# A top-2 router behind linear attention: expert work regrouped from blocks of 128 slots to pairs of 256, with a seven-product second layer

## The chip, the cores and the metric

The kernel runs on one core of one Trainium2 chip. The metric is the device time of one execution in microseconds. The time before is 727.77 us, the median of three runs (725.59 to 728.99). The profile is of one more execution and spans 730.0 us from its first to its last instruction. TensorE does matrix products (the profile splits it into PE, the matmuls, and PEld, the loads of the stationary operand), VectorE (DVE) and ScalarE (ACT) do elementwise work, GpSimd (POOL) here mostly issues indirect transfers, and SyncE (SP) issues the other transfers.

## The reference

Attention with a decaying state comes first, then a layer of eight experts in which each token goes to two. All data are float32.

```python
batch, n_heads, seq, head_dim = (4, 8, 768, 48)
N, D, E, F = (3072, 384, 8, 1024)
# attention
f = 1.0 / (1.0 + np.exp(-f_logit))
for t in range(S):
    state = f[:, :, t, :, None] * state + np.einsum('bhd,bhe->bhde', k[:, :, t], v[:, :, t])
    y[:, :, t] = np.einsum('bhd,bhde->bhe', q[:, :, t], state)
# x: (batch * seq, heads * head_dim)
noisy_logits = x @ w_gate + np.log1p(np.exp(x @ w_noise)) * noise
top2 = np.argpartition(-noisy_logits, 2, axis=1)[:, :2]
# top2_w: softmax over the two
for e in range(E):
    for k in range(2):
        mask = top2[:, k] == e
        h = np.maximum(x[mask] @ w1[e], 0.0)
        out[mask] += top2_w[mask, k, None] * (h @ w2[e])
```

3072 tokens with two experts each make 6144 slots. Each slot needs a first layer of 384 x 1024 and a second of 1024 x 384.

## The kernel before

Attention works on 24 samples (six chunks of 128 positions times four batches), and each sample passes through seven stages in a pipeline. The features `x` of each sample are written to `x_rows` in DRAM. After every four samples the router finds the two experts of each token and writes an entry (token, weight) into the list of each expert, also in DRAM. When half of the tokens are routed, `plan("a", ...)` lays out the first 17 blocks of 128 slots (`NA`) by full lists, so that expert work can start before the rest is routed; `plan("b", ...)` lays out the rest. A remainder of at most 64 slots becomes a half block. The program holds a fixed number of blocks and four half blocks (`NH`), and a conditional part at the end for what does not fit into them.

The loads of `f`, `q`, `k` and `v` go into rings of buffers that are given back when attention is over:

```python
RING = {"f": 5, "q": 4, "k": 4, "v": 6}
pads = {n: [ld.tile([C, H, DP], F32, tag=f"{n}{i}", name=f"{n}{i}") for i in range(RING[n])] for n in "fqkv"}
```

One block of 128 slots; `KO` is 3, `FO` is 8 and `NR` is 2 (two buffers for the weights of each layer, loaded only where the expert changes, `cond=new`):

```python
def turned(t):
    xp = one_bank(f"xgp{t}")
    for i in range(KO):
        nc.tensor.transpose(xp[:, i * 128:(i + 1) * 128], xg[t][:, i * 128:(i + 1) * 128], ident)
    xt[t] = ffn.tile([128, KO, 128], F32, tag="xt", name=f"xt{t}")
    nc.vector.tensor_copy(xt[t], xp[:, 0:DM].rearrange("d (k t) -> d k t", k=KO))

def block_of(t, end=NB - NT):
    ahead("fetch", min(t + 5, end))        # the list entries of the block
    ahead("gather", min(t + 4, end))       # the rows of x they name
    hs = ffn.tile([128, FO, 128], F32, tag="hs", name=f"hs{t}")
    for half in range(2):
        hp = one_bank(f"hp{t}_{half}").rearrange("f (o t) -> f o t", t=128)
        for o in range(FO // 2):
            fo = half * (FO // 2) + o
            for i in range(KO):
                nc.tensor.matmul(hp[:, o, :], lhsT=w1[t % NR][:, i, fo * 128:(fo + 1) * 128],
                                 rhs=xt[t][:, i, :], start=(i == 0), stop=(i == KO - 1))       # L838
        nc.scalar.activation(hs[:, half * (FO // 2):(half + 1) * (FO // 2), :], hp, AF.Relu)   # L840
        if half == 0:
            yield
    ahead(1, min(t + NR + 1, end))         # w1 of a later block
    if t + 1 < end:
        turned(t + 1)
    yield
    yp = one_bank(f"yp{t}")
    for fo in range(FO):
        nc.tensor.matmul(yp[:, 0:DM], lhsT=hs[:, fo, :], rhs=w2[t % NR][:, fo, :],
                         start=(fo == 0), stop=(fo == FO - 1))                                 # L849
        # ... one yield in the middle
    ahead(2, min(t + NR + 1, end))         # w2 of a later block
    ys = ffn.tile([128, DM], F32, tag="ys", name=f"ys{t}")
    nc.vector.tensor_scalar(ys, yp[:, 0:DM], slots[t][:, 1:2].bitcast(F32), None, ALU.mult)    # L855
    nc.gpsimd.indirect_dma_start(out=out, ..., in_=ys, ..., compute_op=ALU.add)                # L856
```

The last line adds the block's rows to `out`, so `out` has to be zeroed first. That is done during attention, one or two row groups per sample:

```python
elif stage is output:
    for m in (n - 2,) if 2 <= n < 18 else (2 * n - 20, 2 * n - 19) if 18 <= n < 22 else ():
        nc.sync.dma_start(out=out[m * 128:(m + 1) * 128, :], in_=zero)
```

The first loads for the experts are spread over turns of the driving loop by a generator, once the first half's entries are written:

```python
for what, until in (("", 6), ("fetch", 2), ("fetch", 4), (1, 1), ("fetch", 5), (2, 1), ("", 4), ("gather", 1),
                    ("gather", 2), (1, 2), ("gather", 3), ("", 3), ("turned", 0), (2, 2), ("gather", 4)):
```

Of the kernel before, what the change touches and what calls it, by code (L numbers as in the profile page):

```python
# [10 lines left out]
F32 = mybir.dt.float32  # L11
# [320 lines left out]
def kernel(  # L332
# [48 lines left out]
    NB = max((2 * N - 65 * n) // 128 + n for n in range(E + 1))  # L381
    NH = 4
    HALF = NCH // 2
    NT = 3
    NA = -(-(2 * HALF * B * C - E * 127) // 128)
# [7 lines left out]
    rest = top.tile([1, 1], I32, tag="rest", name="rest")  # L393
    ctx = whole.enter_context(ExitStack())

    const = ctx.enter_context(tc.tile_pool(name="const", bufs=1))
    rt = ctx.enter_context(tc.tile_pool(name="rt", bufs=2))
    ps2 = ctx.enter_context(tc.tile_pool(name="ps2", bufs=1, space=PSUM))
    ps1 = ctx.enter_context(tc.tile_pool(name="ps1", bufs=6, space=PSUM))
    wk = ctx.enter_context(tc.tile_pool(name="wk", bufs=2))  # L400
    ffn = ctx.enter_context(tc.tile_pool(name="ffn", bufs=3))
    loads = ExitStack()
    ld = loads.enter_context(tc.tile_pool(name="ld", bufs=1))

    def one_bank(name):
        return ps1.tile([128, 512], F32, tag="one", name=name)
# [10 lines left out]
    pads = {n: [ld.tile([C, H, DP], F32, tag=f"{n}{i}", name=f"{n}{i}") for i in range(RING[n])] for n in "fqkv"}  # L417
# [16 lines left out]
    end_of = counting("end_of", [[128, N // 128]], base=128)  # L434
    block = counting("block", [[1, NB]])

# [10 lines left out]
    LR = E * N + 128  # L447
# [42 lines left out]
    xw, puts = [], []  # L490
# [123 lines left out]
    def route(c):  # L614
# [3 lines left out]
        def pause():  # L618
            for _ in range(2 if c < HALF else 1):
                yield  # L620
# [43 lines left out]
        for _ in range(2 if c < HALF else 6):  # L664
            yield from pause()
# [12 lines left out]
        def put(b, r):  # L678
            into = nc.gpsimd.indirect_dma_start(  # L679
# [15 lines left out]
    steer, steer_h = {}, {}  # L695

    def plan(name, n, groups, count):


        def t(shape, tag, dtype=F32):  # L700
            return rt.tile([128] + shape, dtype, tag=tag, name=f"{tag}_{name}", bufs=1)

        total = one_bank(f"total_{name}")[:, 0:E]
        nc.tensor.matmul(total, lhsT=ones, rhs=upto[groups - 1][:, :, B], start=True, stop=True)
        full = t([E, N // 128], "full")
        nc.vector.tensor_tensor(full, total.unsqueeze(2).broadcast_to((128, E, N // 128)),
                                (end_of if count == ALU.is_ge else over_of).unsqueeze(1).broadcast_to((128, E, N // 128)), count)
        yield
        nblk, ends, step = t([E], "nblk"), t([E], "ends"), t([E], "step")
        nc.vector.tensor_reduce(nblk, full, axis=AX.X, op=ALU.add)  # L710
        if count == ALU.is_gt:
            half, first, ends_h = t([E], "half"), t([E], "first"), t([E], "ends_h")
            nc.vector.scalar_tensor_tensor(half, in0=nblk, scalar=128.0, in1=total, op0=ALU.mult, op1=ALU.is_lt)
            nc.vector.scalar_tensor_tensor(first, in0=iota, scalar=float(N // 128), in1=nblk, op0=ALU.mult, op1=ALU.add)
            nc.vector.tensor_tensor_scan(ends_h, data0=ones[:, 0:E], data1=half, initial=0.0, op0=ALU.mult, op1=ALU.add)
        nc.vector.tensor_tensor(nblk, nblk, used[:, 0:E], ALU.subtract)
        nc.vector.tensor_tensor_scan(ends, data0=ones[:, 0:E], data1=nblk, initial=0.0, op0=ALU.mult, op1=ALU.add)
        yield
        if count == ALU.is_gt:
            over = t([1], "over")  # L720
            nc.vector.tensor_scalar(over, ends_h[:, E - 1:E], NH + 0.5, None, ALU.is_gt)
            nc.vector.scalar_tensor_tensor(more, in0=ends[0:1, E - 1:E], scalar=n - NT + 0.5, in1=over[0:1], op0=ALU.is_gt, op1=ALU.max)

        nc.vector.tensor_tensor(step, used[:, 1:E + 1], used[:, 0:E], ALU.subtract)
        nc.vector.tensor_tensor(step, step, nblk, ALU.subtract)
        nc.vector.tensor_scalar(step, step, float(N // 128), None, ALU.add)
        yield
        past = t([NB, E], "past")[:, 0:n, :]
        nc.vector.tensor_tensor(past, block[:, 0:n].unsqueeze(2).broadcast_to((128, n, E)),
                                ends.unsqueeze(1).broadcast_to((128, n, E)), ALU.is_ge)  # L730
        yield
        ex, row, new = t([n], f"ex{n}"), t([n], f"row{n}"), t([n], f"new{n}")
        nc.vector.tensor_reduce(ex, past, axis=AX.X, op=ALU.add)
        nc.vector.tensor_tensor(past, past, step.unsqueeze(1).broadcast_to((128, n, E)), ALU.mult)
        nc.vector.tensor_reduce(row, past, axis=AX.X, op=ALU.add)
        yield
        nc.vector.scalar_tensor_tensor(row, in0=row, scalar=used[:, 0:1], in1=block[:, 0:n], op0=ALU.add, op1=ALU.add)
        nc.vector.tensor_scalar(row, row, float(E * N // 128), 128.0, ALU.min, ALU.mult)
        to = top.tile([128, n, 3], I32, tag=f"steer_{name}", name=f"steer_{name}")
        nc.vector.tensor_copy(to[:, :, 1], row)  # L740
        nc.vector.tensor_scalar(ex, ex, float(E - 1), None, ALU.min)
        nc.vector.tensor_copy(to[:, :, 0], ex)
# [12 lines left out]
        for i in range(n):  # L755
            steer[base + i] = to[0:1, i, :]
# [368 lines left out]
```

## Time and profile before

The table has the groups that the change touches, from the profile of the kernel before. "Mean" is the mean length of one instruction; matmuls overlap their neighbours, so a mean is longer than the distance from one to the next.

| line | engine | what | count | busy us | mean ns |
|---|---|---|---|---|---|
| L838 | PE | first layer, 128 columns | 2304 | 267.7 | 276 |
| L849 | PE | second layer, 384 columns | 768 | 257.3 | 487 |
| L816 | PE | transposes of gathered rows | 144 | 24.0 | 276 |
| L840 | ACT | relu, 128 x 512 | 96 | 57.3 | 597 |
| L818 | DVE | copy of the transposes | 48 | 26.8 | 558 |
| L855 | DVE | scaling by the gate | 48 | 29.6 | 617 |
| L856 | POOL | scatter into `out`, issue | 48 | 76.0 | 1583 |
| L799 | POOL | gather of rows, issue | 48 | 47.9 | 999 |

The weights are 96 conditional loads of 1536 KB each. The zeros are 24 writes of 192 KB. The groups L838 and L849 have 3072 of the 5354 matmul records; an f32 matmul leaves two records. Read the table together with the stretches of the span: the busy shares are means over attention, which ends near 184 us, and over the expert blocks, which begin near 160 us and run to 717 us.

### The profile page before, as it was taken

What the parts mean: (1) busy time and instruction counts of PE and PEld (TensorE: products, weight loads), DVE (VectorE), ACT (ScalarE), POOL (GpSimd) and SP (SyncE); (2) the same over time, 40 slices, a digit from 0 to 9 for tenths busy, and PEclk for the clock granted to TensorE, in tenths of its full rate; (3) what the DMA queues carried; (4) which work ended last, traced back from release to release, by engine and by line L of the source; (5) the groups of instructions that cost most, each with busy time, mean ns of one, the idle gap of its engine ahead of it and who ended that gap; (6) DMA issues with size and microseconds to landing.
All of it is one profiled execution on the core that took longest, in us unless ns stands there. A gap on an engine that the chain in (4) does not pass through costs nothing.

```text
span 730.0 us, 13666 instructions
## 1 busy us (share of the span) xinstructions
PE 699.4 (96%) x5354; PEld 563.0 (77%) x5354; DVE 200.2 (27%) x503; ACT 163.7 (22%) x365; POOL 232.8 (32%) x267
## 2 busy tenths in 40 slices
PE   6999989969999999999999999999999999999992
PEld 5889978858788787787788768876787678767881
DVE  7878887822232250010110110010011001101000
ACT  5766655621111010110010011001110101010100
POOL 5223674421174562122132123312322232312210
PEclk9999999989999999999999999999999999999997
DMA  8889888889997988899839649974997189563211
GB/s 173 151 199 216 166 164 182 165 279 368 373 260 194 251 189 264 282 301 331 276 57 381 195 113 292 351 250 118 302 348 233 26 267 333 161 210 74 34 23 15
DMA packets 179866, 156.41 MB, mean 214 GB/s; under 512 B 116978, under 2 KB 164240, under 8 KB 179792
## 3 DMA queue, kind: packets, MB, share of 16 engines
q1 hardware_dynamic: 167440, 135.91, 62.7%
q0 software_dynamic: 12352, 19.52, 13.2%
q8 instruction: 45, 0.74, 0.4%
q14 instruction: 29, 0.24, 0.1%
HBM read 192.51 MB, written 20.15 MB: 291 GB/s over the span
## 4 chain that ended last, share of the span: by engine, by line
PE 87%; DMA 5%; DVE 3%; ACT 1%; SPq 1%; issue 1%; POOL 0%; POOLq 0%; DVEq 0%; ACTq 0%
PE hp L838 36%; PE yp L849 34%; PE sc L554 3%; PE xgp L816 2%; PE xp L605 2%; PE y L572 2%; PE yp_h L910 1%; PE hp_h L896 1%; DMA k<-in_k_dram 1%; DMA w<-in_moe_w_dram 1%; DMA x_rows<-xs 1%; PE y L583 1%; DVE L L528 1%; PE kp L514 1%; PE kp L548 1%
## 5 line engine op out<-in xcount | busy, mean ns | idle before, releaser
L838 PEld LDWEIGHTS hp<-xt,w 128*128 128x128 f32 x2304 | 264.9, 192 | 15.3 <-issue 3.4
L838 PE MATMUL hp<-xt,w 128*128 128x128 f32 x2304 | 267.7, 276 | 0.4 <-DMA w<-in_moe_w_dram 0.4
L849 PE MATMUL yp<-w,hs 128*128 128x384 f32 x768 | 257.3, 487 | 0.0
L849 PEld LDWEIGHTS yp<-w,hs 128*128 128x128 f32 x768 | 141.7, 190 | 90.0 <-issue 2.6
L856 POOL DMA_INDIRECT out_dram<-ys,slots x48 | 76.0, 1583 | 308.8 <-DVE ys L855 171.4
L840 ACT ACTIVATE hs<-hp 128x512 f32<-128x512 f32 x96 | 57.3, 597 | 455.1 <-PE hp L838 455.1
L818 DVE COPY xt<-xgp 128x384 f32<-128x384 f32 x48 | 26.8, 558 | 236.8 <-PE xgp L816 236.8
L855 DVE TENSOR_SCALAR ys<-yp,slots 128x384 f32<-128x384 f32 x48 | 29.6, 617 | 204.0 <-PE yp L849 199.4
L799 POOL DMA_INDIRECT xg<-x_rows,slots x48 | 47.9, 999 | 35.4 <-DMA slots<-lists 19.1
L679 POOL DMA_INDIRECT lists<-entry,sloti x48 | 47.6, 992 | 12.9 <-issue 9.1
L508 POOL TENSOR_SCALAR f<-f 128x384 f32<-128x384 f32 x22 | 28.0, 1272 | 30.8 <-DMA f<-in_f_logit_dram 17.4
L557 DVE TENSOR_TENSOR A<-sc,causal 128x1024 f32<-128x1024 f32 x24 | 29.3, 1222 | 16.1 <-PE sc L554 15.9
L554 PE MATMUL sc<-qP,kQ 64*128 64x128 f32 x384 | 30.6, 304 | 0.0
L528 DVE TENSOR_TENSOR_SCAN L<-f,cap 128x512 f32<-128x512 f32 x24 | 29.8, 1243 | 2.2 <-ACT cap L523 2.2
L572 PE MATMUL y<-A,v 128*64 128x128 f32 x384 | 28.1, 290 | 1.7 <-DMA v<-in_v_dram 1.4
L816 PE MATMUL xgp<-ident,xg 128*128 128x128 f32 x144 | 24.0, 276 | 5.5 <-DMA xg<-x_rows,slots 5.5
L915 POOL DMA_INDIRECT out_dram<-ys_h,slots_h x8 | 11.4, 1431 | 55.6 <-DVE ys_h L913 48.0
L554 PEld LDWEIGHTS sc<-qP,kQ 64*128 64x128 f32 x384 | 25.7, 204 | 4.3 <-issue 3.8
L605 PE MATMUL xp<-w_rt,yT 128*128 128x112 f32 x192 | 27.2, 284 | 0.0
L572 PEld LDWEIGHTS y<-A,v 128*64 128x64 f32 x384 | 21.9, 143 | 5.6 <-DVE A L557 1.6
L605 PEld LDWEIGHTS xp<-w_rt,yT 128*128 128x128 f32 x192 | 23.3, 191 | 3.6 <-issue 2.2
L587 ACT COPY yT<-y 128x256 f32<-128x256 f32 x48 | 15.5, 376 | 41.7 <-PE y L583 40.3
(169 smaller groups left out, 439.3 us busy)
## 6 DMA issues: line engine op xcount, KB each, us to landing
w<-in_moe_w_dram SPq DMA_DIRECT2D x96, 1536.0 KB
w_h<-in_moe_w_dram SPq DMA_DIRECT2D x8, 1536.0 KB
f<-in_f_logit_dram SPq DMA_DIRECT2D x24, 192.0 KB
q<-in_q_dram SPq DMA_DIRECT2D x24, 192.0 KB
k<-in_k_dram SPq DMA_DIRECT2D x24, 192.0 KB
v<-in_v_dram SPq DMA_DIRECT2D x24, 192.0 KB
x_rows<-xs SPq DMA_DIRECT2D x24, 192.0 KB
out_dram<-zero SPq DMA_DIRECT2D x24, 192.0 KB
```

What stands on the lines that cost most here:

```text
L528: nc.vector.tensor_tensor_scan(L[n], data0=logf[n], data1=cap[n % 2].rearrange("d a t -> d (a t)"), initial=0.0, op0=ALU.add, op1=ALU.min)
L554: nc.tensor.matmul(sc[:, par, cols(hp)], lhsT=kQ[n][rows(par), cols(hp)], rhs=qP[n][rows(par), cols(hp)], start=True, stop=True)
L572: nc.tensor.matmul(at(hp, par), lhsT=vt[:, 2 * hp + par, :], rhs=A[n][:, par, cols(hp)], start=(hp < 2), stop=(c == 0 and hp >= HP - 2))
L605: nc.tensor.matmul(xp[:, hp, :], lhsT=yT[n][:, hp % 2, cols(hp // 2)], rhs=w_rt[:, hp, :], start=True, stop=True)
L679: into = nc.gpsimd.indirect_dma_start(out=lists, out_offset=bass.IndirectOffsetOnAxis(ap=sloti[:, r, b:b + 1], axis=0), in_=entry[:, c, b, ...
L799: nc.gpsimd.indirect_dma_start(out=xg[t], out_offset=None, in_=x_rows[0:HALF * B * C] if t < NA else x_rows, in_offset=bass.IndirectOffset ...
L816: nc.tensor.transpose(xp[:, i * 128:(i + 1) * 128], xg[t][:, i * 128:(i + 1) * 128], ident)
L838: nc.tensor.matmul(hp[:, o, :], lhsT=w1[t % NR][:, i, fo * 128:(fo + 1) * 128], rhs=xt[t][:, i, :], start=(i == 0), stop=(i == KO - 1))
L840: nc.scalar.activation(hs[:, half * (FO // 2):(half + 1) * (FO // 2), :], hp, AF.Relu)
L849: nc.tensor.matmul(yp[:, 0:DM], lhsT=hs[:, fo, :], rhs=w2[t % NR][:, fo, :], start=(fo == 0), stop=(fo == FO - 1))
L855: nc.vector.tensor_scalar(ys, yp[:, 0:DM], slots[t][:, 1:2].bitcast(F32), None, ALU.mult)
L856: nc.gpsimd.indirect_dma_start(out=out, out_offset=bass.IndirectOffsetOnAxis(ap=slots[t][:, 2:3], axis=0), in_=ys, in_offset=None, bounds_ ...
```

## The change

Blocks become pairs of 256 slots. There are 24 of them (`NP`), of which the first five (`NA`) are laid out when half of the tokens are routed. The four half blocks of 64 remain. A remainder of 65 to 192 slots would become a single block of 128 in the conditional part at the end.

The first layer has 256 columns for each matmul. The second layer of a pair is a product of two matrices, each cut into 2 x 2: the activations by halves of the hidden dimension (`f`) and by the two sets of 128 slots (`s`), the weights by halves of the hidden dimension and of the 384 output columns (192 each). Winograd's form of Strassen's method makes it from seven products of the parts instead of eight. It needs four sums of the weights (`u1` to `u4`) and four of the activations (`s1` to `s4`) ahead of the products, and more additions after them. The sums are made on VectorE. The activation sums lie where attention's `f` ring was, the weight sums where the `q` and `k` rings were. The first pair runs while `q` and `k` are still in use, so its weight sums lie in the second buffer of `w1`. The rings become single tiles with a lifetime of the whole program for this.

```diff
+    f_all = ring.tile([C, RING["f"], H, DP], F32, tag="f_all", name="f_all")
+    qk_all = ring.tile([C, RING["q"] + RING["k"], H, DP], F32, tag="qk_all", name="qk_all")
...
+    sm = {i + 1: f_all[:, i].rearrange(...) for i in range(4)}
+    sums_of = [sums(w1[1].rearrange("p k f -> p (k f)")), sums(qk_all.rearrange("p a h d -> p (a h d)"))]
...
-    def block_of(t, end=NB - NT):
+    def pair_of(t):
+        def a(f, s):
+            return hs[:, f * FH:(f + 1) * FH, s * 128:(s + 1) * 128]
+        def b(f, c):
+            return w2[t % NR][:, f * FH:(f + 1) * FH, c * HC:(c + 1) * HC]
+        def mix(*which):
+            for m in which:
+                x, y, op = {"u1": (b(0, 1), b(0, 0), ALU.subtract), "u2": (b(1, 1), u[1], ALU.subtract),
+                            "u3": (b(1, 1), b(0, 1), ALU.subtract), "u4": (b(1, 0), u[2], ALU.subtract),
+                            "s1": (a(0, 1), a(1, 1), ALU.add), "s2": (sm[1], a(0, 0), ALU.subtract),
+                            "s3": (a(0, 0), a(0, 1), ALU.subtract), "s4": (a(1, 0), sm[2], ALU.subtract)}[m]
+                nc.vector.tensor_tensor((u if m[0] == "u" else sm)[int(m[1])], x, y, op)
+        u = sums_of[t > 0]
+        when = [["u3"], ["u1"], ["u2", "s3"] if t else ["u2"], ["u4"]]
+        when += [["s1"], ["s2"], ["s4"]] if t else [["s3", "s1"], ["s2"], ["s4"]]
+        ahead("fetch", t + 5)
+        ahead("gather", t + 3)
+        hs = ffn.tile([128, FO, 256], F32, tag="hs", name=f"hs{t}", bufs=1)
+        for fo in range(0, FO, 2):
+            hp = one_bank(f"hp{t}_{fo}").rearrange("f (o t) -> f o t", o=2)
+            for o in range(2):
+                for i in range(KO):
+                    nc.tensor.matmul(hp[:, o, :], lhsT=w1[t % NR][:, i, ...], rhs=xt[t][:, i, :], ...)
+            nc.scalar.activation(hs[:, fo:fo + 2, :], hp, AF.Relu)
+            mix(*when[fo // 2])
+            if fo == FO - 2 and t:
+                ahead(1, t + NR + 1)
+            yield
+        def product(name, x, y):
+            ...
+            for o in range(FH):
+                nc.tensor.matmul(P[name], lhsT=x[:, o, :], rhs=y[:, o, :], start=(o == 0), stop=(o == FH - 1))
+        product(1, a(0, 0), b(0, 0))
+        ...                                        # mix(*when[4])
+        product(7, sm[3], u[3])
+        nc.scalar.copy(P17.rearrange("t a w -> t (a w)"), bank[0][:, 0:DM])
+        nc.scalar.mul(left[0], P17[:, 0], gate[0])
+        if t + 1 < NP:
+            turned(t + 1, 0)
+        mix(*when[5])
+        yield
+        product(4, a(1, 1), u[4])
+        mix(*when[6])
+        yield
+        product(5, sm[1], u[1])
+        nc.vector.tensor_tensor(left[1], P17[:, 1], P[4], ALU.add)
+        nc.vector.tensor_tensor(right[1], P17[:, 1], P[5], ALU.add)
+        if t + 1 < NP:
+            turned(t + 1, 1)
+        yield
+        product(6, sm[2], u[2])
+        nc.vector.tensor_tensor(mid, P17[:, 0], P[6], ALU.add)
+        for to in (left[1], right[1]):
+            nc.vector.tensor_tensor(to, to, mid, ALU.add)
+        nc.scalar.mul(ys[1], ys[1], gate[1])
+        scatter(1)
+        nc.vector.tensor_tensor(mid, mid, P[5], ALU.add)
+        nc.scalar.mul(right[0], mid, gate[0])
+        yield
+        product(2, a(1, 0), b(1, 0))
+        nc.vector.scalar_tensor_tensor(left[0], in0=P[2], scalar=gate[0], in1=left[0], ...)
+        yield
+        product(3, sm[4], b(1, 1))
+        if not t:
+            ahead(1, NR + 1)
+        ahead(2, t + NR + 1)                       # never ahead of the loads of w1
+        nc.vector.scalar_tensor_tensor(right[0], in0=P[3], scalar=gate[0], in1=right[0], ...)
+        scatter(0)
```

The zeros of the first half's rows are written during attention from sample 8 on, one row group per sample, and those of the second half beside the pairs from pair 1 on, one per piece of a pair. Routing is spread over fewer turns from the second chunk on, and the first loads start from a list of their own:

```diff
-                for m in (n - 2,) if 2 <= n < 18 else (2 * n - 20, 2 * n - 19) if 18 <= n < 22 else ():
-                    nc.sync.dma_start(out=out[m * 128:(m + 1) * 128, :], in_=zero)
+                if 8 <= n < 8 + NS // 2:
+                    zeros(1)
...
-            for _ in range(2 if c < HALF else 1):
+            for _ in range(2 if c == 0 else 1):
...
+        for what, until in (("", 13), ("fetch", 1), (1, 1), ("fetch", 2), ("fetch", 3), (2, 1), ("gather", 1), ("gather", 2),
+                            ("fetch", 4), ("gather", 3), ("fetch", 5), ("turned", 0)):
...
+            for _ in range(2 if i >= NS - 1 else 1):
+                if done["turned"] and (n_first < 5 or i >= NS - 3 and stage is not forget) and (n_first < 11 or i >= NS - 1):
+                    next(pairs)
+                    n_first += 1
```

A pair has eleven pieces (one per `yield`). With the last condition up to two pairs are begun while the last samples of attention still run. After attention its buffers in PSUM are given back[...].

## The prediction

> **What bounds the kernel now.** I read the busy line, the row of 40 slices and the chain of work that ended last first, because together they say whether one engine sets the time.
>
> ```profile
> PE 699.4 (96%) x5354; PEld 563.0 (77%) x5354; DVE 200.2 (27%) x503; ACT 163.7 (22%) x365; POOL 232.8 (32%) x267
> ...
> PE   6999989969999999999999999999999999999992
> ...
> PE 87%; DMA 5%; DVE 3%; ACT 1%; SPq 1%; issue 1%; POOL 0%; POOLq 0%; DVEq 0%; ACTq 0%
> ```
>
> TensorE is busy for 96% of the span and is 87% of the chain. "Busy" is an average, so next I cut the span into stages (columns after the stretch: its length, then PE, PEld, DVE, ACT and POOL busy us, granted clock, DMA share, GB/s):
>
> ```profile
> 20.00:100.00 80.00, 77.67 (x1105) 70.49 (x1104) 64.60 (x140) 55.48 (x145) 33.38 (x43) 1.00 0.88 188
> 100.00:150.00 50.00, 44.69 (x604) 39.25 (x602) 38.05 (x91) 29.29 (x73) 25.43 (x41) 0.97 0.83 164
> 150.00:160.00 10.00, 6.62 (x60) 5.45 (x61) 2.01 (x3) 0.65 (x2) 3.57 (x4) 0.66 0.89 286
> 160.00:340.00 180.00, 180.00 (x1183) 145.84 (x1184) 39.25 (x158) 24.49 (x52) 64.07 (x78) 1.00 0.94 282
> 340.00:717.00 377.00, 377.00 (x2291) 290.23 (x2289) 40.59 (x71) 42.96 (x72) 94.79 (x73) 1.00 0.66 202
> 717.00:730.00 13.00, 0.19 (x1) 0.00 (x0) 0.62 (x1) 0.00 (x0) 1.56 (x1) 0.65 0.15 19
> ```
>
> From 160 to 717 us, 557 us, TensorE has no gap: the expert blocks are bound by it, and only fewer or shorter matmuls shorten them. Before 160 us attention runs, with VectorE (64.60 of 80) and DMA (share 0.88) close behind; here there are gaps. The last 13 us are the last block's scatter and the end of the program.
>
> TensorE's own timeline in the bound stretch (start, length, line, count) gives the price of a block:
>
> ```profile
> 342.99 5.52 PE L838 MATMUL hp<-xt,w 128*128 128x128 f32 x48
> 348.35 0.49 PE L816 MATMUL xgp<-ident,xg 128*128 128x128 f32 x3
> 348.67 5.33 PE L849 MATMUL yp<-w,hs 128*128 128x384 f32 x16
> 353.84 5.52 PE L838 MATMUL hp<-xt,w 128*128 128x128 f32 x48
> ```
>
> Differences of starts: first layer 348.35-342.99 = 5.36 us, transposes 0.32, second layer 5.17, one block 10.85. One f32 matmul is two records (24 matmuls, 48 records), so a record of 128 columns takes 5.36/48 = 111.7 ns and one of 384 columns 5.17/16 = 323 ns. Those two are the ruler for everything below.
>
> Last, the end of attention, where the gaps are:
>
> ```profile
> 146.87 0.60 PE L514 MATMUL kp<-ident,k 128*128 128x128 f32 x4
> 152.94 0.87 PE L816 MATMUL xgp<-ident,xg 128*128 128x128 f32 x3 [5.47 <-DMA xg<-x_rows,slots]
> 153.74 2.08 PE L554 MATMUL sc<-qP,kQ 64*128 64x128 f32 x16
> ...
> 159.87 2.92 PE L838 MATMUL hp<-xt,w 128*128 128x128 f32 x24 [0.44 <-DMA w<-in_moe_w_dram]
> 162.72 1.16 PE L554 MATMUL sc<-qP,kQ 64*128 64x128 f32 x16
> ```
>
> The first block's gather arrives 5.47 us late, and afterwards the same 16 score records take 2.08 us instead of 1.16.
>
> [...] The 2.08 against 1.16 us and the clock of 0.66 agree: a gap costs more than itself. [...] The trace has 689 ns for the 512 elements of qP[...] and 1222 for the 1024 of the masked scores[...]. [...]
>
> **The change part by part.** The work fits: from the reference's inputs the eight experts get 766, 738, 811, 777, 800, 755, 719 and 778 slots, which by the new rule are 3 pairs each and 4 half blocks, exactly 24 pairs and 4 halves. The 48 blocks and 4 halves of the trace become the same slots, and the fallback stays unused.
>
> *First layer.* 24 matmuls of 256 columns in place of 48 of 128. Between my two points a column costs (323-111.7)/256 = 0.825 ns, so a record of 256 takes 217 ns, and a pair 48 x 217 = 10.4 us against 2 x 5.36 = 10.7. Saves 0.3.
>
> *Second layer.* Eight products of four 192-column matmuls per pair (that is what 16 matmuls of 384 columns are) become seven: 28 matmuls, 56 records of 111.7 + 64 x 0.825 = 164.5 ns, 9.2 us against 10.34. Saves 1.1. Columns alone would save 1/8, 1.28; twice as many records give 0.15 back.
>
> *Transposes* stay, 0.65 per pair. A pair: 10.4 + 9.2 + 0.65 = 20.3 us against 21.7. **24 x 1.4 = 34 us saved**, all of it in the gapless stretch or taking its place.
>
> *Sums around the products.* VectorE per pair: four weight sums of 768 elements, [...]3.8; four activation sums of 512, 0.69 each, 2.8; two copies of 0.56, 1.1; eight operations on 192 columns at about 0.35 (the trace's 192-element copy takes 0.345), 2.8. Together 10.5 us in 20.3. ScalarE: four activations of 0.6 plus copies, about 4. Both lie beside TensorE. Latency also fits: weight sums need only w2 and run during the first layer; the s1 sum is ready about 1.7 us after the last first-layer matmul (copy-out 0.6, sum 0.7, waits), while its product starts after three others, 3.9 us later. Price on the path: 0 to 0.2 us per pair.
>
> *Zeros and the start of the experts.* Twelve of the 24 zero writes leave attention. Routing of the first half also takes fewer turns; counting turns of the driving loop, the fetch of the first list moves from near sample 21 to sample 19 and the first transposes come 12 turns (about 1.6 samples, 9.5 us) after it. Before, the first fetch is issued at 147.11 us, next to the 146.87 us end above, so the data could not be there. I expect the gap of 5.5 us and its slow clock (0.9 for the scores, 0.9 for the outputs that follow) mostly to go, and perhaps part of a 2.0 us wait for k at 109 us. **About 7 of 11 us saved.**
>
> *First pair's sums in w1[1].* So pair 1's w1 can be loaded only after the first pair's sixth product. In program order about 7 us of TensorE work lies between that and pair 1. A 1.5 MB weight load takes 4.2 us at the 368 to 373 GB/s that the two best early slices show, and took 8.77 us when it was contended at 151 us. **I charge 3 us** here, with the slower restart.
>
> *End.* Before: VectorE scaling 0.62, scatter issue 1.56, landing. After: a VectorE operation on 192 columns, then the same scatter; the other half's scatter was issued a product earlier. 0.
>
> Sum: 727.8 - 34 - 7 + 3 = 690; with the small terms rounded, **689 us**.
>
> **Rivals.** *A: the sums hold up the products.* If a sum came late in each pair, by 1 to 1.5 us, the 34 us would shrink to nothing: 715 to 720. For it: VectorE goes from a tenth of the late stretch (40.59 of 377) to half,[...] and its queue mixes copies that wait for TensorE with sums that TensorE needs. Against: two to three microseconds of margin in the order above. *B: the weights become the wait.* w1[1] is held by sums, loads of w2 are held back behind those of w1, and four loads come together after pair 0. For it: 8.77 us in the chain for one load before. If the four loads run at a contended pace, TensorE idles 10 to 15 us around pair 1: 700. Later it is unlikely: fewer loads than before (21 expert changes by my count against about 30) and 20 us per pair to land them. *C: attention gains nothing from fewer zeros*, because its other traffic is as heavy: 696. *D: the layers gain as reckoned, and all stalls of the start go*: 680.
>
> **Range and chances.** The 34 us rest on measured record times and a full TensorE; interpolation is good to 2 ns on 2496 records, 5 us. The start may be off by 8. That gives 677 to 705. Faster by over 2% means below 713.2: only A does otherwise. Faster 0.94, within 2% 0.05, slower 0.01.
>
> **What would show it.** Right: second-layer records near 164 ns, 56 to a pair, pair period 20.2 to 20.5 us between first-layer starts, TensorE without gaps after attention, VectorE near 50% in the pairs, no wait above 1 us for xg at the first pair. Wrong: TensorE waiting on VectorE sums in every pair (A), a wait on w of several us at pair 1 (B), or records of 192 columns well above 165 ns. A repeated wait of over 1.4 us per pair would refute the prediction.

## The result and the profile after

The changed kernel takes **706.14 us** (median, 704.01 to 706.79) against 728.38 us (725.59 to 729.51) of the kernel before in the same measurement: a ratio of **0.9695, interval 0.9659 to 0.9731**. It is faster, by 22.2 us. The prediction said 689.

First the busy line, the row of 40 slices and the chain that ended last, from the page of the changed kernel:

```profile
PE 667.0 (95%) x4778; PEld 598.9 (85%) x4778; DVE 383.3 (55%) x860; ACT 208.7 (30%) x461; POOL 239.4 (34%) x267
...
PE   6999989979999989999999999999999999999992
...
issue 12%; DMA 4%; POOL 2%; POOLq 0%
```

TensorE is as full as before, and VectorE has gone from 27% to 55%. The chain breaks off after 18% of the span here, so it says nothing of the rest, and the readings below rest on stretches and timelines.

The stretches of the changed kernel (length, then PE, PEld, DVE, ACT and POOL busy us, granted clock, DMA share, GB/s):

```profile
20.00:100.00 80.00, 77.72 (x1100) 70.19 (x1100) 62.23 (x136) 53.91 (x140) 34.18 (x47) 1.00 0.94 200
100.00:140.00 40.00, 35.76 (x451) 31.92 (x451) 32.90 (x108) 22.18 (x58) 21.83 (x34) 0.91 0.72 144
140.00:150.00 10.00, 6.16 (x82) 5.62 (x83) 5.45 (x12) 4.73 (x12) 5.67 (x8) 0.93 1.02 377
...
160.00:260.00 100.00, 95.96 (x656) 87.19 (x654) 59.39 (x187) 23.62 (x55) 35.90 (x49) 0.98 0.60 182
260.00:400.00 140.00, 140.00 (x759) 126.35 (x758) 67.79 (x127) 29.16 (x54) 45.04 (x34) 1.00 0.77 242
400.00:689.00 289.00, 289.00 (x1579) 258.90 (x1578) 136.46 (x249) 60.78 (x114) 75.30 (x57) 1.00 0.54 157
```

From 260 us on TensorE has no gap. But the stretch of 160 to 260 us, which was full before, has lost 4 us to gaps. Gaps and a lowered granted clock are there from 100 to 160 us as they were before (0.91 from 100 to 140 us and 0.83 from 140 to 160; before, 0.97 from 100 to 150 and 0.66 from 150 to 160). Attention now ends near 211 us, where it ended near 184. TensorE's timeline gives a pair, where it is gapless:

```profile
300.23 10.52 PE L880 MATMUL hp<-xt,w 128*128 128x256 f32 x48
310.59 1.46 PE L894 MATMUL y<-w,hs 128*128 128x192 f32 x8
311.89 1.46 PE L894 MATMUL y<-qk_all,f_all 128*128 128x192 f32 x8
313.19 0.49 PE L839 MATMUL xgp<-ident,xg 128*128 128x128 f32 x3
...
320.35 10.52 PE L880 MATMUL hp<-xt,w 128*128 128x256 f32 x48
```

First layer 310.59 - 300.23 = 10.36 us, one product 1.30, transposes 0.33 twice, **one pair 20.12 us**, against two blocks of 10.85, 21.70, before. A record of 256 columns thus takes 10.36/48 = 215.8 ns and one of 192 columns 1.30/8 = 162.5. The line through these two, 53.3 ns for 64 columns, gives 322.4 ns at 384 columns and 109.2 at 128, where the kernel before took 323 and 111.7.

The sums' groups on the page (count, then busy us, mean ns, idle before and its releaser):

```profile
L867 DVE TENSOR_TENSOR f_all<-hs 128x512 f32<-128x512 f32 x48 | 33.1, 690 | 114.5 <-ACT hs L882 109.4
L867 DVE TENSOR_TENSOR qk_all<-w 128x768 f32<-128x768 f32 x46 | 42.4, 961 | 10.3 <-DMA w<-in_moe_w_dram 10.3
```

They take 690 ns for 512 elements and 961 for 768. The 0.96 us of the prediction for 768 elements was an estimate; midway between the 689 ns for 512 elements and the 1222 for 1024 in the kernel before lie 956. TensorE's 20.12 us are the sum of its own records without a gap, so nothing of the sums is on the path there.

Three waits around the start of the experts, in brackets at the end of the line:

```profile
148.25 0.61 PE L839 MATMUL xgp<-ident,xg 128*128 128x128 f32 x3 [3.65 <-DMA xg<-x_rows,slots]
...
185.41 5.45 PE L880 MATMUL hp<-xt,w 128*128 128x256 f32 x24 [0.17 <-DMA w<-in_moe_w_dram]
...
254.02 2.58 PE L894 MATMUL y<-qk_all,f_all 128*128 128x192 f32 x8 [2.44 <-DVE past_halves_b L725]
```

The first pair's rows still come late, 3.65 us instead of 5.47, and after the wait the granted clock is 0.50 from 150 to 155 us (before, 0.50 from 152 to 157 us). Pair 1's weights, held back by the sums, cost 0.17 us. And in the fourth pair a product waits 2.44 us, after which it takes 2.58 us instead of 1.46 (granted clock 0.72 from 254 to 260 us, and 0.50 in it from 255 to 256 us).

**The ledger.** I take from each trace the moment TensorE ends, less 24 pairs (20.12 us; 21.70 before) and four half blocks (6.81 us in both kernels): what is left is the time outside the pairs. The tail is the part of it after the first pair's (block's) transposes. "Idle" is TensorE's end less its busy time on the page.

| trace | first transposes | TensorE ends | outside the pairs | tail | idle |
|---|---|---|---|---|---|
| before | 152.94 | 717.19 | 169.2 | 16.2 | 17.8 |
| changed | 148.25 | 689.13 | 179.0 | 30.8 | 22.1 |

So the pairs give 24 x 1.58 = 37.9 us, and about 10 us are lost outside them: 4.3 us of idle time, and the rest in longer busy time for the same work. By the timed medians the loss is 15.7 us (37.9 - 22.2); the traced execution of the kernel before took 731.71 us, 3.3 above its median, and that of the changed kernel 704.01, 2.1 below. The prediction had 34 and a gain of 4. The experiments are about that loss.

### The profile page after: what moved, and what is told of

Its sections match the earlier page's. It is cut to its first block, busy times and chain, and to the rows that moved or that the text cites. A ratio compares the mean times of both kernels' runs of the same rounds, so it can differ in the third digit from the quotient of the medians.

```text
span 702.3 us, 12595 instructions
## 1 busy us (share of the span) xinstructions
PE 667.0 (95%) x4778; PEld 598.9 (85%) x4778; DVE 383.3 (55%) x860; ACT 208.7 (30%) x461; POOL 239.4 (34%) x267
## 5 line engine op out<-in xcount | busy, mean ns | idle before, releaser
L880 PE MATMUL hp<-xt,w 128*128 128x256 f32 x1152 | 257.6, 382 | 1.6 <-issue 0.7
L880 PEld LDWEIGHTS hp<-xt,w 128*128 128x128 f32 x1152 | 218.3, 191 | 31.5 <-issue 1.2
L894 PE MATMUL y<-qk_all,f_all 128*128 128x192 f32 x552 | 102.4, 329 | 2.4 <-DVE past_halves_b L725 2.4
L894 PEld LDWEIGHTS y<-qk_all,f_all 128*128 128x128 f32 x552 | 91.2, 191 | 5.1 <-remote 2.7
L894 PE MATMUL y<-w,hs 128*128 128x192 f32 x392 | 72.9, 330 | 0.0
L894 PEld LDWEIGHTS y<-w,hs 128*128 128x128 f32 x392 | 66.0, 192 | 4.3 <-issue 3.2
L867 DVE TENSOR_TENSOR qk_all<-w 128x768 f32<-128x768 f32 x46 | 42.4, 961 | 10.3 <-DMA w<-in_moe_w_dram 10.3
L867 DVE TENSOR_TENSOR qk_all<-w,qk_all 128x768 f32<-128x768 f32 x46 | 43.8, 953 | 0.6
L894 PE MATMUL y<-w,f_all 128*128 128x192 f32 x216 | 39.8, 327 | 0.0
L1007 POOL DMA_INDIRECT out_dram<-ys_h,slots_h x8 | 11.7, 1459 | 80.4 <-DVE ys_h L1005 73.2
L894 PEld LDWEIGHTS y<-w,f_all 128*128 128x128 f32 x216 | 35.6, 190 | 0.3 <-issue 0.3
L516 POOL TENSOR_SCALAR f_all<-f_all 128x384 f32<-128x384 f32 x22 | 26.9, 1224 | 20.6 <-DMA f_all<-in_f_logit_dram 13.3
```

The source lines that it names most:

```text
L516: engine.tensor_scalar(raw, raw, XMIN, None, ALU.max)
L867: nc.vector.tensor_tensor((u if m[0] == "u" else sm)[int(m[1])], x, y, op)
L880: nc.tensor.matmul(hp[:, o, :], lhsT=w1[t % NR][:, i, (fo + o) * 128:(fo + o + 1) * 128], rhs=xt[t][:, i, :], start=(i == 0), stop=(i == K ...
L894: nc.tensor.matmul(P[name], lhsT=x[:, o, :], rhs=y[:, o, :], start=(o == 0), stop=(o == FH - 1))
```

## The experiments

"Control" is the changed kernel unchanged, measured beside the others; comparisons are with the control of the same measurement. A sample begins with the first matmul of its features (L613; L605 before). **Theory A** at first: pairs do what was reckoned, and the loss is made by program order at the start of the experts. **Theory B**, the rival: the sums, or loads and zeros, take the time.

### The controls

> The changed kernel once more, unchanged, with a new profile. Theory A (my reading): TensorE lost its time at fixed places, set by the order of the program: near 101, 122, 145 and 251 us; then the same gaps (2.6, 1.2, 3.9 and 2.6 us, and the slow clock after them) come back within 2 us of those places, and the time is 704 to 708. Rival B: the gaps are chance of the transfers in flight; then at least two of the four are gone or elsewhere in this profile, with the time still 703 to 708.

> The changed kernel unchanged, as the yardstick for the three beside it on the same chip. Both theories: between 701 and 707 us, the ratio to the kernel before between 0.962 and 0.972, and the large gap ahead of the first pair's transposes (3.7 to 4.0 us so far) there again.

> The changed kernel unchanged, the yardstick on this chip. Ratio to the kernel before 0.957 to 0.972 as so far. TensorE's time after the first pair's transposes, less 24 pairs of 20.12 us and 4 half blocks of 6.81 us, was 23.7 to 30.8 us in its traces (16.3 in the kernel before): the same range here.

> The changed kernel unchanged, the yardstick on this chip: ratio to the kernel before 0.957 to 0.970. Pair 5's rows (the first from the whole lists) land within 2 us of the moment TensorE turns to them, as in all traces so far.

> The changed kernel unchanged, the yardstick for the run beside it. Two kinds of traces of it have been seen: with VectorE and ScalarE starting 1 to 5 us after the TensorE result they wait for, at some places between 94 and 253 us (spans 697 to 704 us), and without (692 and 693 us). Either kind can come here.

| control | us | ratio and interval | first transposes | outside the pairs | tail | idle | loss by the medians |
|---|---|---|---|---|---|---|---|
| e1_again | 701.71 | 0.9636 (0.961 to 0.9662) | 147.20 | 174.4 | 27.2 | 20.6 | 10.5 |
| e1_control2 | 695.66 | 0.9587 (0.9565 to 0.9609) | 145.14 | 168.8 | 23.7 | 20.0 | 8.6 |
| e1_control3 | 694.57 | 0.9641 (0.9601 to 0.9681) | 144.90 | 170.1 | 25.2 | 18.2 | 11.7 |
| e1_control4 | 705.92 | 0.9649 (0.9619 to 0.9678) | 148.20 | 180.7 | 32.5 | 25.1 | 12.7 |
| e1_control5 | 703.41 | 0.9648 (0.9617 to 0.968) | 148.37 | 180.9 | 32.6 | 25.8 | 12.2 |

The wait ahead of the first transposes is there every time (3.5 to 4.4 us), so it belongs to the program and is not chance. The gap near 251 us is not: it is missing in e1_again, e1_control2 and e1_control3, and the times that were expected of e1_again and e1_control2 did not come. The times vary by 11 us from one measurement to another; the kernel before varies too (720.8 to 731.1), so the ratios differ by less than the times. The last column is 37.9 less the gain over the kernel before in the same measurement. With the first result it is 8.6 to 15.7 us: the loss is there in all six, so the miss of the prediction is not chance either.

Behind this lie two kinds of traces. They differ in ScalarE's timeline at the same place of the program, first in the changed kernel, then in e1_control2:

```profile
98.25 0.57 ACT L558 COPY kn<-kp 128x512 f32<-128x512 f32 x1
103.05 0.65 ACT L595 COPY yT<-y 128x256 f32<-128x256 f32 x2 [4.23 <-remote]
```

```profile
96.99 0.57 ACT L558 COPY kn<-kp 128x512 f32<-128x512 f32 x1
98.87 0.65 ACT L595 COPY yT<-y 128x256 f32<-128x256 f32 x2 [1.32 <-PE y L591]
```

In the second the copy starts on TensorE's result. In the first it starts 4.6 us after the result is there by the records, and the profile names no releaser ("remote"). I call these late starts. In the traces of the changed kernel, e1_again, e1_control4 and e1_control5 there are 7 to 9 of them of about 1 to 5 us, between 80 and 255 us; in e1_control2, e1_control3 and the one trace of the kernel before, no start is over 0.9 us late without another reason named. They come with the measurement: all ten traces taken with e1_again, e1_control4 and e1_control5 have them, and none of the eight taken with e1_control2 and e1_control3. The chip alone doesn't make the difference, since e1_control2 and e1_control4 ran on the same one. And the loss doesn't rest on them: without them the part outside the pairs is still 169 to 170 us, no less than before, and the loss by the medians 8.6 and 11.7 us.

### e3_eight_products: pairs, but a plain second layer

```diff
-        product(1, a(0, 0), b(0, 0)) ... product(3, sm[4], b(1, 1))
+        # for s in (1, 0), for fo in range(FO): 16 matmuls of 384 columns, and no sums
+                nc.tensor.matmul(halves[s][:, 0:DM], lhsT=hs[:, fo, s * 128:(s + 1) * 128], rhs=w2[t % NR][:, fo, :], ...)
```

> Pairs of 256 slots kept, all else of the change kept, but the second layer done by the plain product: 16 matmuls of 384 columns for a pair, no sums, one scaling per 128 slots. Theory A (the seven products give their full reckoned saving, 24 x (10.32 - 9.10) = 29 us, and the rest of the change costs some 7 us): 733 to 737, slower than the kernel before. Rival C (the sums on VectorE cost TensorE about 0.6 us a pair, or more): 715 to 722. Rival D (sums also disturb attention and routing): the gaps near 101 and 251 us vanish here, time 725 to 730.

734.61 us, ratio 1.007 (1.0044 to 1.0096), 32.9 us above its control (e1_again). Its timeline has the pair:

```profile
380.41 10.52 PE L880 MATMUL hp<-xt,w 128*128 128x256 f32 x48
...
401.75 10.52 PE L880 MATMUL hp<-xt,w 128*128 128x256 f32 x48
```

21.34 us. So the wider first layer is worth 0.36 us of a pair and the seven products 1.22, together the 1.58. This is theory A of the run (733 to 737 us). Its outside part is 181 us, no less than in its control (174.4): the loss is there without any sum, and theory B falls as far as the sums go. Without the seven products the rest of the change is a small loss.

### e2_gathers_first: the gathers ahead of the weight loads

```diff
-("fetch", 1), (1, 1), ("fetch", 2), ("fetch", 3), (2, 1), ("gather", 1), ("gather", 2),
+("fetch", 1), ("fetch", 2), ("gather", 1), ("gather", 2), (1, 1), ("fetch", 3), (2, 1),
```

> In the list of first loads the gathers of the first pair are issued ahead of the two weight loads (1.5 MB each). Theory A: the gather was late (3.65 us wait at 145 us, then half clock)[...]; then that wait falls under 1 us and the time falls by 3 to 5 us against the changed kernel, to about 702. Rival B: the weights then come late instead and TensorE waits as long for w1 at the first pair's first matmul; time unchanged within 1.5 us.

705.66 us, ratio 0.966 (0.9623 to 0.9697), beside 0.9636 of its control: no gain. The wait at the first transposes is 2.7 us in two parts, and the profile no longer names the rows as its end; VectorE and ScalarE start 5.5 us late there (151.8 us). But the edit moved less than it set out to: SyncE issues the first weight load at 139.91 us and GpSimd the gather only at 141.47, so just the second load (142.49) has gone behind it. Whether the gather is slowed by the weights therefore stays open.

### e4_slow_routing: routing at its old pace

```diff
-            for _ in range(2 if c == 0 else 1):      # and 2 if c == 0 else 6
+            for _ in range(2 if c < HALF else 1):    # and 2 if c < HALF else 6
```

> Only the pacing of the router for the second and third chunk is put back to that of before (two turns for each step instead of one). Theory A: the squeezed routing made the losses at 101 and 122 us[...]; then attention up to sample 17 is 4 to 6 us earlier, but the first pair starts about 1.3 samples later, so pair work is moved, not lost: time 701 to 706. Rival B: the losses there have nothing to do with routing: gaps stay, and the later start of the pairs costs 0 to 5 us: 706 to 711.

714.58 us, ratio 0.979 (0.9763 to 0.9818), 12.9 us above its control. Sample 14 begins at 110.69 us (114.76 in the control), so the quicker routing does slow attention. But what comes after pays more for the old pace, as TensorE's timeline shows:

```profile
156.49 0.87 PE L839 MATMUL xgp<-ident,xg 128*128 128x128 f32 x3 [6.52 <-DMA xg<-x_rows,slots]
...
211.57 1.74 PE L894 MATMUL y<-w,hs 128*128 128x192 f32 x8 [3.78 <-ACT hs L882]
```

The first transposes come 9 us later, the tail is 33.5 us, and TensorE is idle for 31.1 us before its end, against 20.6 in the control. The quicker routing is worth 13 us on balance; it isn't the fault. Neither expected time (701 to 711 us) came.

### e9_route1_slow: only the second chunk at its old pace

```diff
-            for _ in range(2 if c == 0 else 1):      # and 2 if c == 0 else 6
+            for _ in range(2 if c <= 1 else 1):      # and 2 if c <= 1 else 6
```

> Only the second chunk's routing is given back its old pace (two turns to a step); the third keeps the new one. Theory A (squeezed routing is what stalls attention at 80 and 101 us): both gaps vanish, sample 14 begins 4 to 5 us earlier than in the control, sample 18 still 2 to 4 us earlier, and the time falls by 2 to 4 us. Theory B (the gaps only come at another place, since the third chunk's routing then follows on the second's): sample 18 begins no earlier than in the control and the time is within 1.5 us of it or above.

696.57 us, ratio 0.9601 (0.9579 to 0.9624), 0.9 us above e1_control2. The gap of 1.3 us at 82 us is gone, but sample 14 begins no earlier (113.16 us, 112.94 in the control), and the first transposes come at 146.78 instead of 145.14, with a wait of 5.3 instead of 4.4. That is theory B of this run.

### e5_zeros_before: all zeros in attention again

```diff
-                if 8 <= n < 8 + NS // 2:
-                    zeros(1)
+                zeros(1 if 2 <= n < 18 else 2 if 18 <= n < 22 else 0)
```

> All 24 zero writes back in attention, as in the kernel before; all else as changed. If spreading the zeros is worth what the prediction supposed, the DMA share in attention rises and the waits there with it: 2 to 5 us slower than the control. If the zeros are hidden anyway (rival C), within 1.5 us of the control; attention's first half, to sample 12, then begins its samples within 1 us of the control's.

699.9 us, ratio 0.9652 (0.9626 to 0.9679), 4.2 us above e1_control2. Attention is not slowed (sample 12 begins at 97.90, 98.77 in the control). The wait for the first pair's rows is longer, here from the wait list of this run (us in total, times, longest):

```profile
PE xgp L839 <- DMA xg<-x_rows,slots: 6.8, 1, 6.8
```

4.42 us in the control. SyncE issues the first list's fetch at 137.43 us instead of 134.56; from the gather's issue to the transposes it is 7.1 us, no longer than the control's 7.6. After the longer wait the granted clock is 0.66 from 140 to 160 us, where the control has 0.83 and then 1.00 (over the whole span 0.982 and 0.989). TensorE's idle time in all is the same (19.6 and 20.0). So spreading the zeros is worth about 4 us, but not through the gather: this trace has a later fetch and a lower clock, and how the zeros bring them about is not shown.

### e8_turn_later: the first transposes six turns later

```diff
-("fetch", 4), ("gather", 3), ("fetch", 5), ("turned", 0)):
+("fetch", 4), ("gather", 3), ("fetch", 5), ("", 6), ("turned", 0)):
```

> The first pair's transposes are placed six turns (about 5 us of attention) later, the gather and all loads stay where they are. Theory A (the handover is the failed term: the gather is asked for too shortly before TensorE's program reaches the transposes, and the wait is pure loss): the 3.7 to 4 us gap and the 1.0 us gap after it vanish, with them the half clock, and the time falls by 4 to 6 us against the control. Theory B (what is saved there is given back, since the pair's matmuls were filling gaps of attention and now come later): the gap vanishes and the time stays within 1.5 us of the control.

703.46 us, ratio 0.9701 (0.968 to 0.9722): **7.8 us slower** than e1_control2. The wait for the rows is gone; two others stand in its place:

```profile
183.14 2.83 PE L880 MATMUL hp<-xt,w 128*128 128x256 f32 x12 [2.98 <-DMA w<-in_moe_w_dram]
...
269.04 0.90 PE L839 MATMUL xgp<-ident,xg 128*128 128x128 f32 x3 [4.57 <-DMA xg<-x_rows,slots]
```

The first is pair 1's `w1`, whose buffer holds the first pair's sums: rival B of the prediction, hidden until then. The second is a **second hand-over**. Pair 5 is the first from the whole lists and waits for attention's last routing. Only five pairs come from the first half's lists, about 100 us of work, where the kernel before had 17 blocks, 184 us. In e1_control3 its last gather is issued at 257.4 us and takes about 6, and TensorE turns to it at 264.03 without a wait: hardly any slack. VectorE's sums and additions hold up products of the first pairs by another 3.5 us (1.25, 0.66 and 1.59). In all, TensorE is idle for 25.5 us, 20.0 in the control: neither theory of this run foresaw that.

### e10_even and e11_even_more: pairs laid evenly beside attention's last samples

```diff
-if done["turned"] and (n_first < 5 or i >= NS - 3 and stage is not forget) and (n_first < 11 or i >= NS - 1):
+if done["turned"] and stage not in (summed, decays) and (n_first < 11 or i >= NS - 1):   # e10_even
+if done["turned"] and stage not in (summed, decays):                                     # e11_even_more
```

> The first pair's eleven pieces are laid between attention's stages as the kernel before laid its blocks (five to a sample, without the hold after the fifth piece), pair 1 still waits for the last sample. Theory A (the failed term is the tail of attention: with fewer pieces of experts beside it, attention's last samples run at their own slow pace): the tail shrinks by 2 to 4 us against the control, and so does the time. Theory B (the tail is long because the pair's operands come late, VectorE with sums and attention's work at once): no gain or a loss, with waits for f_all or hs at the products.

> As the run with the first pair laid evenly, but pairs 1 and 2 follow at once, five pieces to a sample, as the kernel before had it. Theory A: the tail falls from 24 to 31 us to about 16 to 19 us, and the time by 6 to 10 us against the control. Theory B (the first pair's sums keep pair 1's w1 out, so that there is nothing to lay beside attention at that moment): a wait for w of 3 to 8 us at pair 1 while attention still runs, and the time within 2 us of the control or above.

704.38 us, ratio 0.9782 (0.9742 to 0.9822), and 704.62 us, ratio 0.9785 (0.9748 to 0.9821): 10 us slower than e1_control3. The expectation that the thin interleaving makes the long tail fell; the tail grows from 25.2 to 37.7 us in e10_even and 34.5 in e11_even_more. The waits of e11_even_more:

```profile
185.06 2.83 PE L880 MATMUL hp<-xt,w 128*128 128x256 f32 x12 [1.62 <-DMA w<-in_moe_w_dram]
...
271.90 0.90 PE L839 MATMUL xgp<-ident,xg 128*128 128x128 f32 x3 [3.88 <-DMA xg<-x_rows,slots]
```

The same two as in e8_turn_later; e10_even has them too (2.0 and 4.2 us).

### e6_routing_off_products: the last routing only beside first layers

```diff
-        for _ in range(1 if 3 <= piece < 7 else 3):
+        for _ in range(0 if 3 <= piece < 8 else 4):
```

> The routing's last steps and list entries, after attention, are kept out of the pieces in which the second layer's products run, and come four to a piece beside the first layer. If VectorE's routing steps in front of the sums are what holds up TensorE at 235 to 255 us, the gaps there (0.9 and 2.6 us in the first trace, with a half clock after the second) vanish and the time falls by 1 to 4 us against the control. If these stalls are of the list entries themselves or chance, the gaps come elsewhere and the time is within 1.5 us.

700.24 us, ratio 0.9714 (0.9672 to 0.9755), 5.7 us slower than e1_control3. A routing matmul waits 2.0 us at 235 us, and pair 5's rows come 2.7 us late. Slower last routing is paid for at the second hand-over. The gaps that this run was to mend are missing in its control, so it tells nothing of their cause.

### e13, e14, e15: a faster last routing, alone and with the two mends

```diff
-        for _ in range(1 if 3 <= piece < 7 else 3):
+        for _ in range(4):
```

> After attention the routing of the last chunks and its list entries run four steps to every piece of pair work, instead of three, and one during four pieces. Theory A (two hand-overs of about equal length: the first pair's rows, and pair 5's rows from the whole lists): pair 5's rows land 5 to 10 us before TensorE wants them, but TensorE had no wait there in the control, so the time moves less than 2 us either way. Theory B (VectorE is short beside the sums): waits for f_all, qk_all or past at the products, and 2 to 5 us slower than the control.

> The first pair's transposes six turns later (which alone lost 7.8 us on its chip against the control), with the faster last routing. Theory A (the second hand-over took the gain away): the 4.6 us wait for pair 5's rows and its half clock vanish, the time falls by 4 to 8 us against the transposes-later run, to within 3 us of the control, and the w1 wait of 3 us at pair 1 is what is left. Theory B (it was lost elsewhere): 6 us or more above the control, as without the faster routing.

> Pairs 0 to 2 laid evenly beside attention (which alone lost 10 us on its chip against the control), with the faster last routing. Theory A: the 3.9 us wait for pair 5's rows vanishes, the time falls 4 to 8 us, to 2 to 6 us above the control; the 1.6 us wait for w1 at pair 1 stays. If it ends below the control, laying pieces evenly was worth something after all. Theory B: no better than 8 us above the control.

Alone: 706.1 us, ratio 0.965 (0.9618 to 0.9681), as its control (e1_control4). Pair 5's gather is issued at 260.2 us and TensorE comes to it at 276.5, so there are some 10 us of slack now, and they buy nothing, as expected. With evenly laid pairs: 716.13 us, ratio 0.9792 (0.9759 to 0.9824), 10.2 us above the control, no better than e11_even_more was to its own. The wait for pair 5's rows is gone, but TensorE waits for VectorE's routing instead, in its timeline:

```profile
252.85 0.19 PE L1066 MATMUL count<-ones,low 128*1 128x1 f32 x2 [4.58 <-DVE low L1062]
```

So the second hand-over is one of several ties, not the one cause: theory A of this run fell. (e15 has late starts, e11_even_more has none, so the waits of the two compare only roughly.) The third, e14, can't be used: one execution took 714 us, which is 8 above the control, and five took 729 to 732, one of which is the traced one, with two late starts of 9 us. ScalarE and VectorE there:

```profile
159.15 0.37 ACT L595 COPY yT<-y 128x256 f32<-128x256 f32 x1 [10.66 <-remote]
```

```profile
163.41 1.02 DVE L840 COPY xt<-xgp 128x384 f32<-128x384 f32 x2 [11.94 <-remote]
```

TensorE had finished the two results at 149.82 and 154.02 us, 9 us before these starts.

### e16_entries_apart: list entries of the later chunks further apart

```diff
-if puts and (slot % 3 == 0 or n_routed >= HALF):      # after attention: one put with each routing step
+if puts and (slot % 3 == 0 or n_routed == HALF):      # after attention: one put for each piece
```

> GpSimd's list entries of the last three chunks are set apart: every third turn in attention's last part instead of every turn, and one to a piece of pair work instead of one to three; those of the first three chunks stay as they are and serve as a check within the run. Theory A (TensorE's signals come late where list entries follow on each other every 1.27 us): if the control shows late starts, those at 94 to 104 us stay and those at 150 to 165 and 236 to 255 us vanish, and the time falls by 2 to 5 us. Theory B (the lateness has nothing to do with the entries): late starts of 1 to 5 us stay in both stretches, and the time is within 2 us of the control. If the control shows none, nothing is told of the signals, and the time is within 2 us either way, or above if pair 5's rows come later.

704.56 us, ratio 0.9661 (0.9628 to 0.9694), beside 0.9648 of e1_control5. The late starts at 94 and 103 us stay, those at 237 to 240 us vanish, those at 252 to 255 us stay, and one of 5 us is new at 131 us. But after 239 us the entries still came 1.25 us apart, as GpSimd was behind. The late starts that are left lie in such a run of entries or within 2 us of its end, which fits theory A; yet e1_control2 and e1_control3 have the same runs of entries and no late start. Undecided.

## Why the prediction was right and wrong

**Faster, with the pairs as the reason: right.** Pair period 20.12 us against 20.3, VectorE at 47% in the pairs (136.46 of 289 us; half was forecast), sums off the path, no gap from 260 us on, and no gain at all with a plain second layer (e3_eight_products). The 34 us were 37.9: the line between two points put a record of 256 columns at 217 ns (215.8) and one of 192 at 164.5 (162.5), 0.17 us of a pair and 4 us in all. Its point at 128 columns (111.7) lies 2.5 ns above the line through the new points at 192 and 256 (109.2).

**"I charge 3 us" for pair 1's weights: mis-sized.** 0.17 us. The load had time because attention's last samples lie between. Where they were filled otherwise (e8, e10, e11), 1.6 to 3.0 us appeared, about what was charged.

**"About 7 of 11 us saved": this step failed**, and it is the miss. The 11 us agree with TensorE's idle time from 20 to 160 us in the kernel before (2.33, 5.31 and 3.38 us by its stretches). Nothing of it went: it is 11.1 us in the changed kernel and 10.9 to 13.5 in the controls. Three things were wrong in the step.

*The wait didn't go.* The step set "12 turns, 9.5 us" between the first list's fetch and the transposes against the data's way. These are the fetch and the gather in the kernel before, then the same with the two weight loads in the changed one:

```profile
147.11 2.90 SPq L790 DMA_DIRECT2D slots<-lists  x4
149.63 1.06 POOL L799 DMA_INDIRECT xg<-x_rows,slots  x1 [6.82 <-DMA slots<-lists]
```

```profile
136.60 0.39 SPq L811 DMA_DIRECT2D slots<-lists  x1
137.98 0.38 SPq L830 DMA_DIRECT2D w<-in_moe_w_dram  x1
140.94 0.37 SPq L832 DMA_DIRECT2D w<-in_moe_w_dram  x1
141.17 1.07 POOL L822 DMA_INDIRECT xg<-x_rows,slots  x1 [0.27 <-issue]
```

TensorE is there at 144.6 us (148.25 less its wait), so the turns took 8.0 us. The way of list and rows took until 148.25, 11.7 us, where it had taken 5.8 before (147.11 to 152.94). Program order makes 2.1 us of the difference: the gather is issued 4.6 us after the fetch (2.5 before). The gather makes the rest, 7.1 us from its issue to the transposes instead of 3.3. It now follows both weight loads, where it went ahead of them before (150.97 us); whether they slow it is not shown.

*An earlier hand-over is not time saved.* It came 4.7 us earlier, 8 in the two control traces without late starts. But TensorE does attention too, and what it had not done by then it had to do later: before, sample 19 had begun (145.45) when the experts started; now sample 18 begins after it (148.66). In e1_control2 the two cancel: transposes 7.8 us earlier, a tail 7.5 us longer, and of that tail only 1.5 us idle (0.4 before). Attention left over is not all of it, though: in e4_slow_routing sample 19 had begun too (147.95), and the tail is 33.5 us, with 12.5 us idle in it. And an idle stretch taken away is a gain only if no other comes: e8_turn_later took the whole wait away, about 10 us of others came, and the time rose.

*New ties were not seen.* With five pairs from the first half's lists where 17 blocks had been, the last routing comes just in time, and VectorE, with sums to make, is at the same moment routing. The runs that mend one place (e8, e10, e11, e15) break another.

The measures named in the step did help: the zeros are worth 4.2 us and the quicker routing 12.9, both against the same kernel without them, some 17 us if the two add. The start is 8.6 to 15.7 us slower all the same, so the pairs must cost more there than the 3 us that the prediction charged. This is inferred: the kernel before was not run with the quicker routing. **How that cost divides**, between longer pieces, fewer early pairs and two gathers for a start, **stays open**: no run had early blocks of 128 beside late pairs. Late starts add to the time outside the pairs (174 to 181 us with them, 169 to 170 without), but the kernel before is slower in the same measurements, so the loss hardly follows them.

**Rivals.** A is refuted: TensorE has no gap from 260 us on, and the pair's 20.12 us are all records. B lay hidden. Its number (700) came nearest to 706.14, by luck: pair 1's weights cost 0.17 us. C (696) had a wrong reason, since the fewer zeros do gain. D is refuted: the stalls of the start stayed.

## What to carry to other kernels

A price for each instruction, taken from a gapless stretch and multiplied out, held to 4 us in 520; a saving reckoned at a hand-over between two phases of the same engine did not hold at all. There, count the idle time of the engine over the whole start, follow the data's whole way (list, gather, landing) in microseconds rather than turns, and look for the next hand-over: larger units of work mean fewer that are ready early. If mending a wait makes the kernel slower, list the waits again, since the next one was hidden behind it.

## What the runs showed of the hardware

The late starts were not expected. By the records VectorE or ScalarE begins 1 to 5 us, in e14 about 9 us, after the TensorE result it waits for, and the records of TensorE's signals come in a burst at the end (in the changed kernel at 103.02, 103.08 and 103.17 us, for matmuls that ended at 98.42, 98.43 and 99.51). GpSimd was issuing list entries at or just before such times (from 97.17 to 104.56 us in the same trace), yet the same entries also pass without it in all eight traces of two measurements. The cause is not settled.

A gap costs more than itself after the change too: after the 2.44 us wait at 254.02 us the products take 2.58 and 2.15 us instead of 1.46, at a granted clock of 0.59 from 254 to 256 us and 0.56 from 256 to 258.
